# A linear-attention block with a feed-forward layer, rewritten into one written instruction order

## The chip, the cores and the metric

The kernel runs on one core of one Trainium2 chip. The metric is the device time of one execution in microseconds (us). Before the change it was 351.17 us, the median of five runs (350.06 to 351.9).

The engines are PE (matmul; PEld is its weight load, which overlaps it), DVE (the vector engine), ACT (the scalar engine), POOL (the general-purpose engine) and SP (which issues DMAs). Lines such as L338 refer to the source of the kernel that the profile belongs to. In the changed kernel L299 is a projection (V or K), L338 the K normalisation, L378 the Q projection, L417 the attention matmul, L478 the output projection, L552 the feed-forward up projection and L570 the down projection. A few experiments shift these numbers by a few lines; the names of the tiles stay.

## The reference

The input has 2048 tokens of 640 values, 32 heads of 20, and a hidden width of 1728. Everything is bf16 at the borders.

```
xn = layernorm(x);  q, k, v = xn @ wqkv            # 32 heads of 20
pq = q @ w_phi ; pk = k @ w_phi                    # per head, 20x20
phi_q = [softmax(pq), softmax(-pq)]                # 40 features per head
phi_k = [softmax(pk), softmax(-pk)]
kv = phi_k^T @ v ;  z = sum over tokens of phi_k
o = (phi_q @ kv) / (phi_q @ z + 1e-6)
h = x + o @ wo
out = h + silu(layernorm(h) @ w1) @ w2
```

## The kernel before

It works in stages over 16 tiles of 128 tokens. First it folds w_phi into the Q and K weights, with transposes of the weights on PE. Then comes the K pass:

```
psv = Xn @ Wv ; psk = Xn @ Wfk                     # PE, 640 wide, as 512 + 128 columns
Ek[..., 0:20] = exp(+psk), exp(-psk)               # ACT, heads padded from 20 to 32
nc.vector.tensor_reduce(Sk[:], Ekb[:, :, 0:DH], axis=AX.X, op=ALU.add)       # L258
nc.vector.reciprocal(Sk[:], Sk[:])                                           # L259
nc.vector.tensor_tensor(Ekb[:, :, 0:DH], ..., Sk broadcast, op=ALU.mult)     # L260
for p in range(16):
    nc.tensor.matmul(kv[:, p, 0:42], Ek[:, p*128:(p+1)*128], Vp[:, p, 0:42]) # 2 heads each
... (cut)
```

The Q pass does the same normalisation for Q (L369 to L371), transposes the 2048 padded exponentials with 16 PE transposes and two ACT copies (L388, L398), multiplies by kv, divides, transposes again, applies `wo`, adds the residual as further matmuls against the identity, and normalises. After the Q pass the feed-forward part runs alone, in four blocks of 512 tokens: up projection, ACT sigmoid, DVE multiply by its input, down projection, DVE addition. The framework's scheduler orders the instructions of every engine.

The softmax here doesn't subtract the row's maximum and nothing guards it: scores larger than these inputs give would overflow.

Of the kernel before, what the change touches and what calls it, by code (L numbers as in the profile page):

```python
# [10 lines left out]
AX = mybir.AxisListType  # L11

BF16 = mybir.dt.bfloat16
F32 = mybir.dt.float32


@with_exitstack
def kernel(
# [14 lines left out]
    T = 16  # L33
    S = T * P
# [5 lines left out]
    FC = 14  # L40
    EPS = 1e-5

    x_t = A_x.rearrange("b (t p) d -> p (b t) d", p=P)
    out_t = out.rearrange("b (t p) d -> p (b t) d", p=P)

    persist = ctx.enter_context(tc.tile_pool(name="persist", bufs=1))
    early = ctx.enter_context(ExitStack())
    lnp = early.enter_context(tc.tile_pool(name="ln1", bufs=1))
    fp_ = early.enter_context(tc.tile_pool(name="fold", bufs=1))
    fps = early.enter_context(tc.tile_pool(name="foldps", bufs=2, space=bass.MemoryType.PSUM))  # L50
    lns = early.enter_context(tc.tile_pool(name="ln1s", bufs=3))
    lnps = early.enter_context(tc.tile_pool(name="ln1ps", bufs=2, space=bass.MemoryType.PSUM))
# [3 lines left out]
    eps_t = persist.tile([P, 1], F32, name="eps_t")  # L56
    nc.gpsimd.memset(eps_t[:], EPS)
    nhalf_t = persist.tile([P, 1], F32, name="nhalf_t")
    nc.gpsimd.memset(nhalf_t[:], -0.5)

    wqkv_sb = fp_.tile([P, C, 3 * D], BF16, name="wqkv_sb")
    wqkv_v = A_wqkv.rearrange("(c p) n -> p c n", p=P)
    nc.sync.dma_start(wqkv_sb[:, :, 1 * D : 2 * D], wqkv_v[:, :, 1 * D : 2 * D])
    WPH = fp_.tile([DH, H, DH], BF16, name="WPH")
    nc.scalar.dma_start(WPH[:], A_w_phi.rearrange("h d f -> d h f"))
    X_sb = lnp.tile([P, T, D], BF16, name="X_sb")
    for g4 in range(4):
        nc.gpsimd.dma_start(
            X_sb[:, 4 * g4 : 4 * (g4 + 1), :], x_t[:, 4 * g4 : 4 * (g4 + 1), :]
        )  # L70
    for i in (2, 0):
        nc.sync.dma_start(wqkv_sb[:, :, i * D : (i + 1) * D], wqkv_v[:, :, i * D : (i + 1) * D])
    wo_sb = persist.tile([P, C, D], BF16, name="wo_sb")
    nc.sync.dma_start(wo_sb[:], A_wo.rearrange("(c p) n -> p c n", p=P))
    XT = persist.tile([P, C, S], BF16, name="XT")
    for c in range(C):
        nc.sync.dma_start_transpose(XT[:, c, :], A_x[0, :, c * P : (c + 1) * P])

    SID = fp_.tile([DH, 3 * P], BF16, name="SID")
    nc.gpsimd.memset(SID[:], 0.0)  # L80
    nc.vector.tensor_copy(SID[:, P : P + DH], ident[0:DH, 0:DH])
    phi_sb = fp_.tile([P, C, D], BF16, name="phi_sb")
    for r in range(C):
        pphi = fps.tile([P, H, 32], F32, name="psw")
        heads = []
        for h in range(H):
            r0 = DH * h
            if r0 // P != r and (r0 + DH - 1) // P != r:
                continue
            p0 = r0 - r * P  # L90
            heads.append((h, p0))
        for (h, p0) in heads:
            nc.tensor.matmul(
                pphi[:, h, 0:DH],
                SID[:, P - p0 : 2 * P - p0],
                WPH[:, h, :],
                start=True,
                stop=True,
            )
        h_lo = heads[0][0]  # L100
        h_hi = heads[-1][0] + 1
        if h_lo > 0:
            nc.gpsimd.memset(phi_sb[:, r, 0 : DH * h_lo], 0.0)
        if h_hi < H:
            nc.gpsimd.memset(phi_sb[:, r, DH * h_hi : D], 0.0)
        nc.scalar.copy(
            phi_sb[:, r, DH * h_lo : DH * h_hi].rearrange("p (h f) -> p h f", f=DH),
            pphi[:, h_lo:h_hi, 0:DH],
        )

    Wfq = persist.tile([P, C, D], BF16, name="Wfq")
    Wfk = persist.tile([P, C, D], BF16, name="Wfk")
    Wv = persist.tile([P, C, D], BF16, name="Wv")
    XnT = persist.tile([P, C, S], BF16, name="XnT")

    nc.vector.tensor_copy(Wv[:], wqkv_sb[:, :, 2 * D : 3 * D])

    WTs = {}
    for which in (1, 0):
        base = which * D  # L120
        WT = fp_.tile([P, C, D], BF16, name=f"WT{which}")
        for r in range(C):
            pwt = fps.tile([P, C, P], BF16, name="pwt")
            for ce in range(C):
                nc.tensor.transpose(  # L125
                    pwt[:, ce, :],
                    wqkv_sb[:, ce, base + r * P : base + (r + 1) * P],
                    ident[:],
                )
            nc.scalar.copy(WT[:, r, :], pwt[:].rearrange("p a b -> p (a b)"))  # L130
        WTs[which] = WT

    Xn = lnp.tile([P, T, D], BF16, name="Xn")

    def ln1_group(g):
        for tt in range(8):
            t = g * 8 + tt
            stats = lns.tile([P, 2, 6], F32, name="st1")
            for i in range(2):
                nc.vector.bn_stats(stats[:, i, :], X_sb[:, t, i * 320 : (i + 1) * 320])  # L140
            mv = lns.tile([P, 2], F32, name="mv1")
            nc.vector.bn_aggr(mv[:], stats[:])
            rstd = lns.tile([P, 1], F32, name="rstd1")
            nc.vector.tensor_scalar_add(rstd[:], mv[:, 1:2], EPS)
            nc.gpsimd.tensor_tensor(rstd[:], rstd[:], nhalf_t[:], op=ALU.pow)
            nmr = lns.tile([P, 1], F32, name="nmr1")
            nc.vector.tensor_scalar(
                out=nmr[:], in0=mv[:, 0:1], scalar1=rstd[:, 0:1], scalar2=-1.0,
                op0=ALU.mult, op1=ALU.mult,
            )  # L150
            nc.vector.tensor_scalar(
                out=Xn[:, t, :], in0=X_sb[:, t, :],
                scalar1=rstd[:, 0:1], scalar2=nmr[:, 0:1],
                op0=ALU.mult, op1=ALU.add,
            )
        for c in range(C):
            pst = lnps.tile([P, 8, P], BF16, name="pXT")
            for tt in range(8):
                t = g * 8 + tt
                nc.tensor.transpose(pst[:, tt, :], Xn[:, t, c * P : (c + 1) * P], ident[:])  # L160
            if g == 0:
                nc.vector.tensor_copy(
                    XnT[:, c, g * 8 * P : (g + 1) * 8 * P],
                    pst[:].rearrange("p a b -> p (a b)"),
                )
            else:
                nc.scalar.copy(
                    XnT[:, c, g * 8 * P : (g + 1) * 8 * P],
                    pst[:].rearrange("p a b -> p (a b)"),
                )  # L170

    def fold(which):
        Wf = Wfk if which == 1 else Wfq
        WT = WTs[which]
        for ce in range(C):
            psw = fps.tile([P, D], F32, name="psw")
            for n0, n1 in ((0, 512), (512, 640)):
                for r in range(C):
                    nc.tensor.matmul(  # L179
                        psw[:, n0:n1],  # L180
                        WT[:, r, ce * P : (ce + 1) * P],
                        phi_sb[:, r, n0:n1],
                        start=(r == 0),
                        stop=(r == C - 1),
                    )
            if which == 1:
                nc.scalar.copy(Wf[:, ce, :], psw[:])
            else:
                nc.vector.tensor_copy(Wf[:, ce, :], psw[:])  # L189

    ln1_group(0)
    fold(1)
    fold(0)
    ln1_group(1)
    early.close()

    wpool = ctx.enter_context(tc.tile_pool(name="wpool", bufs=1))
    w1_sb = wpool.tile([P, C, F], BF16, name="w1_sb")
    nc.sync.dma_start(w1_sb[:], B_w1.rearrange("(c p) n -> p c n", p=P))
    w2_sb = wpool.tile([P, FC, D], BF16, name="w2_sb")  # L200
    nc.sync.dma_start(
        w2_sb[:, 0:13, :], B_w2[0 : 13 * P].rearrange("(c p) n -> p c n", p=P)
    )
    nc.sync.dma_start(w2_sb[0:64, 13, :], B_w2[13 * P : F, :])
    HnT = wpool.tile([P, C, S], BF16, name="HnT")

    KVBD = persist.tile([P, 16, 42], BF16, name="KVBD")
    nc.vector.memset(KVBD[:], 0.0)
    p2pre_ctx = ctx.enter_context(ExitStack())
    p2pre = p2pre_ctx.enter_context(tc.tile_pool(name="p2pre", bufs=1))  # L210
    p1ctx = ctx.enter_context(ExitStack())
# [10 lines left out]
    def p1_stage_AB(t):  # L222
# [11 lines left out]
        for n0, n1 in ((0, 512), (512, 640)):  # L234
# [29 lines left out]
            op=ALU.mult,  # L264
        )
        ek_state[t] = Ek
        vp_state[t] = Vp

    def p1_stage_C(t):
        Ek = ek_state[t]  # L270
# [364 lines left out]
```

## Time and profile before

| stretch of the span (us) | what runs | PE busy | DVE busy | granted PE clock |
|---|---|---|---|---|
| 0 to 49 | loads, fold, LayerNorm | 32.58 of 49 | 33.02 | 1.00 |
| 62 to 118 | K pass | 50.03 of 56 | 54.24 | 1.00 |
| 118 to 213 | Q pass | 78.53 of 95 | 85.25 | 0.96 |
| 213 to 350.5 | feed-forward | 131.45 of 137.5 | 52.46 | 1.00 |

The table is taken from this view of the kernel before: busy time of each engine in stretches of the span. The columns are the stretch, its length, then each engine's busy us with its number of instructions in brackets, the granted clock, the mean busy share of the DMA engines, and GB/s.

```profile
core 0: us, PE busy (x) PEld busy (x) DVE busy (x) ACT busy (x) POOL busy (x), PEclk, DMA share, GB/s
0.00:49.00 49.00, 32.58 (x273) 20.33 (x274) 33.02 (x106) 14.95 (x25) 22.47 (x47) 1.00 0.64 175
...
62.00:118.00 56.00, 50.03 (x551) 29.04 (x548) 54.24 (x52) 32.73 (x50) 14.71 (x22) 1.00 0.17 63
118.00:213.00 95.00, 78.53 (x947) 52.93 (x948) 85.25 (x165) 67.16 (x89) 21.28 (x27) 0.96 0.01 2
213.00:350.50 137.50, 131.45 (x755) 61.45 (x753) 52.46 (x74) 39.34 (x62) 0.39 (x1) 1.00 0.06 20
```

The share of DVE moves from stage to stage, so no single engine bounds the kernel: DVE is the busiest in the K and Q passes, PE in the feed-forward part. The page of the kernel before says the same in its slices (the span in 40 equal parts, each digit the busy share in tenths) and in the chain of waits.

```profile
PE   2299878999996779788999767999999999999995
...
DVE  0985987999999999998989865441453145315421
```

```profile
PE 49%; DVE 33%; ACT 6%; DMA 4%; POOL 4%; issue 2%; SPq 0%; DVEq 0%; POOLq 0%; ACTq 0%
```

These are the groups of instructions of the kernel before that the change is about. After the bar come busy us and the mean ns of one, then idle time just before them.

```profile
L260 DVE TENSOR_TENSOR Ek<-Ek,Sk 128x1280 bf16<-128x1280 bf16 x16 | 23.7, 1483 | 1.4
L258 DVE TENSOR_REDUCE Sk<-Ek 128x64 f32<-128x1280 bf16 x16 | 23.6, 1476 | 2.4 <-ACT Ek L256 2.4
...
L371 DVE TENSOR_TENSOR Eq<-Eq,Sq 128x1280 bf16<-128x1280 bf16 x14 | 20.8, 1483 | 0.1
L369 DVE TENSOR_REDUCE Sq<-Eq 128x64 f32<-128x1280 bf16 x14 | 20.5, 1473 | 0.0
...
L388 ACT COPY EqT<-psT 128x1024 bf16<-128x1024 bf16 x16 | 16.3, 1017 | 11.7 <-PE psT L387 11.7
```

One tile of the K pass costs DVE 1.48 + 0.55 + 1.48 us, 3.51 us, and the step from one tile to the next in the chain is about 3.6 us, so DVE hardly pauses.

### The profile page before, as it was taken

What the parts mean: (1) busy time and instruction counts of PE and PEld (TensorE: products, weight loads), DVE (VectorE), ACT (ScalarE), POOL (GpSimd) and SP (SyncE); (2) the same over time, 40 slices, a digit from 0 to 9 for tenths busy, and PEclk for the clock granted to TensorE, in tenths of its full rate; (3) what the DMA queues carried; (4) which work ended last, traced back from release to release, by engine and by line L of the source; (5) the groups of instructions that cost most, each with busy time, mean ns of one, the idle gap of its engine ahead of it and who ended that gap; (6) DMA issues with size and microseconds to landing.
All of it is one profiled execution on the core that took longest, in us unless ns stands there. A gap on an engine that the chain in (4) does not pass through costs nothing.

```text
span 350.5 us, 6366 instructions
## 1 busy us (share of the span) xinstructions
PE 304.0 (87%) x2642; PEld 170.8 (49%) x2642; DVE 235.2 (67%) x407; ACT 165.0 (47%) x239; POOL 62.0 (18%) x101
## 2 busy tenths in 40 slices
PE   2299878999996779788999767999999999999995
PEld 2166445555554556555665443445544544444443
DVE  0985987999999999998989865441453145315421
ACT  3153049646466566776899455420742044104400
POOL 7430552333320012333231010000000000000000
PEclk9999999999999989999999899999999999999999
DMA  8995002910000000000000000001000100010011
GB/s 271 401 197 109 2 1 82 392 35 2 2 0 2 1 2 2 2 0 2 3 2 1 2 0 2 0 21 37 19 2 19 39 19 1 21 38 18 2 37 37
DMA packets 18997, 15.98 MB, mean 46 GB/s; under 512 B 11482, under 2 KB 17818, under 8 KB 18970
## 3 DMA queue, kind: packets, MB, share of 16 engines
q1 hardware_dynamic: 17744, 12.95, 12.7%
q0 software_dynamic: 576, 2.62, 1.8%
q8 instruction: 20, 0.33, 0.4%
q10 hardware_dynamic: 650, 0.03, 0.1%
q14 instruction: 7, 0.06, 0.1%
HBM read 10.35 MB, written 2.62 MB: 37 GB/s over the span
## 4 chain that ended last, share of the span: by engine, by line
PE 49%; DVE 33%; ACT 6%; DMA 4%; POOL 4%; issue 2%; SPq 0%; DVEq 0%; POOLq 0%; ACTq 0%
PE psy L587 19%; PE psh L569 17%; DVE Ek L260 6%; DVE Sk L258 6%; DMA wqkv_sb<-in_A_wqkv_dram 4%; DVE Sq L369 4%; PE psw L179 4%; PE psa L442 3%; DVE O L419 3%; DVE Sk L259 2%; DVE Eq L371 2%; DVE st L485 2%; POOL rstd L490 2%; PE psT L395 1%; PE psq L349 1%
## 5 line engine op out<-in xcount | busy, mean ns | idle before, releaser
L587 PE MATMUL psy<-w_sb,shT 128*128 128x512 bf16 (+2 forms) x448 | 73.0, 300 | 0.0
L569 PE MATMUL psh<-HnT,w_sb 128*128 128x512 bf16 (+1 forms) x280 | 67.4, 378 | 2.4 <-DVE shT L578 1.7
L578 DVE TENSOR_TENSOR shT<-psh,sg 128x512 bf16<-128x512 f32 (+1 forms) x56 | 38.6, 691 | 38.3 <-ACT sg L577 38.3
L577 ACT ACTIVATE sg<-psh 128x512 bf16<-128x512 f32 (+1 forms) x56 | 33.3, 597 | 65.7 <-PE psh L569 57.8
L587 PEld LDWEIGHTS <-shT 128*128 128x128 bf16 (+1 forms) x448 | 33.7, 97 | 35.2 <-issue 10.4
L569 PEld LDWEIGHTS <-w_sb 128*128 128x128 bf16 (+1 forms) x280 | 26.7, 98 | 36.3 <-issue 8.4
L595 DVE TENSOR_TENSOR o_t<-psy,H_sb 128x640 bf16<-128x640 f32 x16 | 13.2, 825 | 43.4 <-PE psy L587 43.4
L442 PE MATMUL psa<-wo_sb,OT 128*128 128x512 bf16 (+1 forms) x160 | 29.4, 314 | 0.5 <-ACT OT L434 0.5
L236 PE MATMUL p1mm<-Wfk,XnT 128*128 128x512 bf16 (+1 forms) x160 | 26.4, 298 | 1.2 <-ACT Ek L256 0.4
L226 PE MATMUL p1mm<-Wv,XnT 128*128 128x512 bf16 (+1 forms) x160 | 25.0, 299 | 1.1 <-DVE Wfq L189 1.0
L349 PE MATMUL psq<-Wfq,XnT 128*128 128x128 bf16 (+1 forms) x140 | 24.0, 298 | 2.0 <-ACT Eq L362 1.7
L258 DVE TENSOR_REDUCE Sk<-Ek 128x64 f32<-128x1280 bf16 x16 | 23.6, 1476 | 2.4 <-ACT Ek L256 2.4
L260 DVE TENSOR_TENSOR Ek<-Ek,Sk 128x1280 bf16<-128x1280 bf16 x16 | 23.7, 1483 | 1.4
L388 ACT COPY EqT<-psT 128x1024 bf16<-128x1024 bf16 x16 | 16.3, 1017 | 11.7 <-PE psT L387 11.7
L255 ACT ACTIVATE Ek<-p1mm 128x640 bf16<-128x640 f32 x16 | 11.3, 704 | 20.5 <-PE p1mm L236 17.2
L371 DVE TENSOR_TENSOR Eq<-Eq,Sq 128x1280 bf16<-128x1280 bf16 x14 | 20.8, 1483 | 0.1
L369 DVE TENSOR_REDUCE Sq<-Eq 128x64 f32<-128x1280 bf16 x14 | 20.5, 1473 | 0.0
L359 POOL MEMSET Eq<- 128x768 bf16 x14 | 10.3, 744 | 56.0 <-PE psT L395 50.5
L140 DVE BATCH_NORM_STATS2 st<-X_sb 128x6 f32<-128x320 bf16 x32 | 14.3, 465 | 8.1 <-DMA X_sb<-in_A_x_dram 8.1
L398 ACT COPY EqT<-psT 128x1024 bf16<-128x1024 bf16 x16 | 16.2, 1016 | 7.3 <-PE psT L395 7.2
L490 POOL TENSOR_TENSOR rstd<-rstd,nhalf_t 128x1 f32<-128x1 f32 x16 | 13.5, 846 | 34.8 <-DVE rstd L489 34.5
L125 PE MATMUL pwt<-ident,wqkv_sb 128*128 128x128 bf16 x50 | 6.7, 307 | 13.7 <-DMA wqkv_sb<-in_A_wqkv_dram 13.0
(91 smaller groups left out, 457.8 us busy)
## 6 DMA issues: line engine op xcount, KB each, us to landing
X_sb<-in_A_x_dram POOLq DMA_DIRECT2D x4, 640.0 KB, 9.4
out_dram<-o_t SPq DMA_DIRECT2D x16, 160.0 KB, 1.8
wqkv_sb<-in_A_wqkv_dram SPq DMA_DIRECT2D x3, 800.0 KB, 11.0
w_sb<-in_B_w_dram SPq DMA_DIRECT2D x1, 2160.0 KB, 8.2
w_sb<-in_B_w_dram SPq DMA_DIRECT2D x1, 2080.0 KB, 13.9
wo_sb<-in_A_wo_dram SPq DMA_DIRECT2D x1, 800.0 KB, 16.6
XT<-in_A_x_dram SPq DMA_TRANSPOSE x5, 5.4
w_sb<-in_B_w_dram SPq DMA_DIRECT2D x1, 80.0 KB, 13.5
```

Of the source, the lines that this page charges most:

```text
L226: nc.tensor.matmul(psv[:, n0:n1], XnT[:, c, t * P : (t + 1) * P], Wv[:, c, n0:n1], start=(c == 0), stop=(c == C - 1),)
L236: nc.tensor.matmul(psk[:, n0:n1], XnT[:, c, t * P : (t + 1) * P], Wfk[:, c, n0:n1], start=(c == 0), stop=(c == C - 1),)
L258: nc.vector.tensor_reduce(Sk[:], Ekb[:, :, 0:DH], axis=AX.X, op=ALU.add)
L260: nc.vector.tensor_tensor(Ekb[:, :, 0:DH], Ekb[:, :, 0:DH], Sk[:].unsqueeze(2).to_broadcast([P, 64, DH]), op=ALU.mult,)
L349: nc.tensor.matmul(psq[:, n0:n1], XnT[:, c, t * P : (t + 1) * P], Wfq[:, c, n0:n1], start=(c == 0), stop=(c == C - 1),)
L369: nc.vector.tensor_reduce(Sq[:], Eqb[:, :, 0:DH], axis=AX.X, op=ALU.add)
L371: nc.vector.tensor_tensor(Eqb[:, :, 0:DH], Eqb[:, :, 0:DH], Sq[:].unsqueeze(2).to_broadcast([P, 64, DH]), op=ALU.mult,)
L442: nc.tensor.matmul(psa[:, n0:n1], OT[:, c, :], wo_sb[:, c, n0:n1], start=(c == 0), stop=False,)
L569: nc.tensor.matmul(psh[0:rows, :], w1_sb[:, c, fc * P : fc * P + rows], HnT[:, c, q * 512 : (q + 1) * 512], start=(c == 0), stop=(c == C - 1),
L577: nc.scalar.activation(sg[0:rows, :], psh[0:rows, :], AF.Sigmoid)
L578: nc.vector.tensor_tensor(shT[0:rows, fc, :], psh[0:rows, :], sg[0:rows, :], op=ALU.mult)
L587: nc.tensor.matmul(psy[:, n0:n1], shT[0:rows, fc, si * P : (si + 1) * P], w2_sb[0:rows, fc, n0:n1], start=(fc == 0), stop=(fc == FC - 1),)
```

## The change

The kernel is rewritten. Its intent is to take work off PE and DVE, and to fill every gap of PE with work of another stage. The core of the diff, with cuts:

```diff
+ORDER = """
+mk st.1 st.0 rs.1 xn.1 rs.0 xn.0 xt.0 xc.0.v st.2 xt.1 xc.1 vp.0 vc.0 vp.1 vc.1 wt.0 wc.0.a st.3
+... (cut: one word for each operation of each tile, about 60 lines)
+"""
 # K normalisation: heads stay 20 wide, and the multiply moves to POOL
-nc.vector.tensor_tensor(Ekb[:, :, 0:DH], ..., Sk broadcast, op=ALU.mult)
+n = H if t == T - 1 else 2 * H           # the last tile is shared with DVE
+nc.gpsimd.tensor_tensor(Ek3[:, 0:n], Ek3[:, 0:n], Sk broadcast, op=ALU.mult)
 # K.V: 64 columns of Ek against 4 heads of V, 20 matmuls of 84 columns a tile
-nc.tensor.matmul(tgt[:, pi, 0:42], Ek[:, p*P:(p+1)*P], Vp[:, p, 0:42], ...)
+nc.tensor.matmul(kv[s][lo:lo+64, r], Ek[:, s, 64*q:64*q+64], Vp[:, HQ[q]:HQ[q]+4, :], ...)
 # Q: exponentials made transposed, so no transposes and no normalisation of Q
+nc.tensor.matmul(ps[:, k, :], Wfq[:, c, r*P:(r+1)*P], XnT[g][:, c, :], ...)       # qp
+nc.scalar.activation(E[:, s, ...], ps, AF.Exp, scale=1.0 - 2.0 * s)               # qe
 # attention for one half of the heads; the two softmaxes are combined afterwards (DVE)
+nc.tensor.matmul(ps[:, s, ...], EqT[g][:, s, r, i*P:(i+1)*P], KVBD[:, s, r, ...])  # dp
+w = sum0/sum1 ; u = A1*w + A0                                                     # dw
+o = u[..., 0:20] * (1/u[..., 20])                                                 # do
 # residual on DVE, with the sum for the LayerNorm; the squares on ACT
-nc.tensor.matmul(psa[:, c_lo:c_hi], XT[:, c, ...], ident[...])
+nc.vector.scalar_tensor_tensor(out=Xv, in0=ps, in1=Xv, ..., accum_out=st[:, 0:1])  # oa
+nc.scalar.activation(sq[:], X[:, t, :], AF.Square, accum_out=st[:, 1:2])           # sq
 # some transposes go through DRAM (words xs/xd, ts/td, hs/hd), the others stay on PE
+nc.sync.dma_start(os_[:], o) ; nc.sync.dma_start_transpose(ot[:], os_[:])
 # feed-forward
-sigmoid on ACT, multiply on DVE
+nc.scalar.activation(sh, ps, AF.Silu)
+# the last chunk of 64 rows is padded with zeros to 128
+# 14 matmuls on zeros run while the first loads are under way
+with tc.manual_schedule(engines={PE, SP, POOL, DVE, ACT}):
+    for word in ORDER.split(): ops[name](*args)
```

Each engine executes its instructions in the order of the words. In that order, feed-forward operations (up, ua, yp, yo) stand among the attention operations of later tiles.

## The prediction

> **What bounds the kernel now.** Stages with different limits. The table of busy time by stretch shows: 0 to 49 us (loads, folding, LayerNorm) PE busy only 33; 62 to 118 us, the K pass, DVE 54.2 of 56; 118 to 213 us, the Q pass, DVE 85.3 of 95; then the FFN, PE 131 of 138. The chain of waits agrees: PE 49%, DVE 33%, ACT 6%. In the K pass the chain is a DVE loop of about 3.6 us a tile: reduce 1.48, reciprocal 0.55, broadcast multiply 1.48. In the Q pass DVE, ACT and PE hand work around through short buffers.
>
> In the chain ten 512-column matmuls take 2.22 us, so PE streams about 2.35 columns a nanosecond. I count 625,000 columns, an estimated 264 us: some 85 of 350 us are PE idleness.
>
> **What the change does.** A rewrite in one hand-fixed instruction order.
> - PE columns fall to about 575,000 (my count), an estimated 240 to 244 us: Q's exponentials are made already transposed (33,000 go); the fold uses only non-zero head blocks (32,000 to 7,000); the residual is added on DVE (10,000 less); some transposes go to DMA. K.V grows to 27,000, attention to 25,000.
> - DVE loses the K multiply (23.7 us, to POOL) and the Q normalisation (reduce 20.5, reciprocal 7.4, multiply 20.8), replaced by combining both halves after the matmul, an estimated 1.9 us per half tile, 61 us. DVE falls from 235 to roughly 160 us.
> - ACT loses the sigmoid step (one Silu), the 32 transposed copies (32.5 us) and H copies; it gains squares.
> - POOL gains the K multiply. The Trainium skill, "GPSIMD Engine Reference", section 3.1, states about 2.6 cycles per element at 1.2 GHz for a two-input op; 1280 elements make an estimated 2.8 us. The old trace has no such instruction. 15.5 of them are 43 us, plus small ops.
>
> **Critical path, by stage.** First real PE work at about 8 us (the first weight landed at 6.2 before), first K projection about 21 us. PE then has 55 us of K-pass work, but POOL, from its first multiply (about 26 us), needs 54: the pass, with the masked KV copies on DVE, ends near 84 us against 118; PE loses some 8 us. The rest is about 408,000 columns, 174 us; with FFN work interleaved into attention I allow 9 us of stalls. The tail (last add and store), about 4 us, stays. 84 + 174 + 9 + 4 = 271 us.
>
> **Prediction: 271 us, 259 to 290 in 8 of 10 cases.** Faster by over 2%: 0.98; within 2%: 0.01; slower: 0.01.
>
> **What would show each step.** Table of engines: fewer PE instructions, DVE about 160 us, POOL well over 100. Groups by line: the POOL multiply near 2.8 us; no 128x1024 ACT copies. Slices: PE at 9 in nearly all slices after 84 us. Chain of waits: PE over 75%, POOL between 26 and 84 us, DVE under 10%. First attention matmul near 84 us.
>
> **What would make it wrong.** A POOL multiply at 3.5 us, or DVE and POOL slowing each other, would cost 10 us or more; at 2 us the K-pass stall vanishes. The 18 round trips through DRAM for transposes share one in-order queue (before, a transpose of 16 blocks held it about 5.6 us); if it blocks, PE idles in the FFN. A denser PE could be granted a lower clock (mean 0.99; 0.96 in the Q pass). The start, some 20 us of small dependent steps, could be slower.

## The result

The changed kernel takes 262.04 us, the median of 8 runs (261.81 to 262.91), against 351.21 us. The ratio is 0.7461 with a 95% interval from 0.7447 to 0.7476. A ratio is always the mean time of one kernel's fast runs over that of the other's fast runs of the same rounds, so it is not quite the ratio of the medians.

This is the stretch view of the changed kernel, cut where its stages begin: the first K projection (21.8 us), the first attention matmul (81.4 us), and the last matmul (257.4 us).

```profile
0.00:21.80 21.80, 16.81 (x139) 10.51 (x140) 15.12 (x42) 10.42 (x15) 11.72 (x43) 1.00 0.97 323
21.80:81.40 59.60, 55.75 (x669) 38.01 (x667) 44.09 (x67) 43.00 (x64) 50.79 (x63) 1.00 0.26 70
81.40:257.40 176.00, 175.47 (x1295) 115.75 (x1295) 97.42 (x255) 65.62 (x94) 22.25 (x80) 1.00 0.21 59
257.40:261.20 3.80, 0.00 (x0) 0.00 (x0) 0.82 (x1) 0.00 (x0) 0.00 (x0) 0.95 0.12 43
```

After 81.4 us PE is busy 175.47 of 176.00 us, while attention and feed-forward work of different tiles alternate. The slices of the changed kernel show the same, and the granted clock stays at the top digit in all of them:

```profile
PE   7789998999997999999999999999999999999994
...
DVE  4689999377648894689787333994735605332012
...
PEclk9999999999999999999999999999999999999999
```

DVE is at 9 in eight of the 40 slices. PE busy went from 304.0 to 248.0 us and PE idle from 46.5 to 13.2 us (span less busy). Busy time includes modelled pipeline ends, so the split is rough. DVE busy went from 235.2 to 157.5 us, ACT from 165.0 to 119.0, and POOL from 62.0 to 84.8. The K reduce is still there, the multiply is now on POOL, and no group for the Q normalisation remains:

```profile
L338 POOL TENSOR_TENSOR Ek<-Ek,Sk 128x1280 bf16<-128x1280 bf16 x15 | 35.0, 2356 | 0.8 <-DVE Sk L331 0.8
...
L328 DVE TENSOR_REDUCE Sk<-Ek 128x64 f32<-128x1280 bf16 x16 | 23.4, 1460 | 7.5 <-ACT Ek L320 7.4
```

Finally, these are the longest waits of PE in the changed kernel: who waited for whom, us in total, times, longest.

```profile
PE mm L417 <- DVE KVBD L370: 1.8, 1, 1.8
PE q L245 <- DVE xn L234: 1.8, 2, 1.5
PE q L599 <- POOL ident masks.py:199: 1.5, 1, 1.5
PE mm L299 <- ACT Vp L309: 1.3, 1, 1.3
PE kv L351 <- POOL Ek L338: 0.6, 1, 0.6
```

KVBD is the masked copy of the K.V sums that the attention matmuls read. PE waits for POOL's multiply only 0.6 us in all. The chain of waits of this profile could not be read as hoped: it is followed back only to 160 us, and its shares add up to 38% of the span (PE 31%).

### The profile page after: what moved, and what is told of

It reads as the page before. It is cut to its first block, busy times and chain, and to the rows that moved or that the text cites. A ratio compares the mean times of both kernels' runs of the same rounds, so it can differ in the third digit from the quotient of the medians.

```text
span 261.2 us, 5215 instructions
## 1 busy us (share of the span) xinstructions
PE 248.0 (95%) x2099; PEld 164.3 (63%) x2099; DVE 157.5 (60%) x363; ACT 119.0 (46%) x172; POOL 84.8 (32%) x186
## 5 line engine op out<-in xcount | busy, mean ns | idle before, releaser
L552 PE MATMUL mm<-HnT,w 128*128 128x512 bf16 (+1 forms) x350 | 63.7, 337 | 0.0
L570 PE MATMUL mm<-w,shT 128*128 128x320 bf16 x448 | 63.5, 299 | 0.0
L570 PEld LDWEIGHTS <-shT 128*128 128x128 bf16 x448 | 43.5, 98 | 16.8
L563 ACT ACTIVATE shT<-mm 128x1024 bf16<-128x1024 f32 (+1 forms) x29 | 28.4, 992 | 54.0 <-PE mm L552 53.8
L552 PEld LDWEIGHTS <-w 128*128 128x128 bf16 x350 | 33.6, 98 | 23.6 <-issue 0.2
L299 PEld LDWEIGHTS <-XnT 128*128 128x128 bf16 x320 | 30.4, 98 | 14.1 <-issue 2.0
L338 POOL TENSOR_TENSOR Ek<-Ek,Sk 128x1280 bf16<-128x1280 bf16 (+1 forms) x16 | 36.9, 2329 | 2.1 <-DVE Sk L331 2.1
L299 PE MATMUL mm<-wv,XnT 128*128 128x320 bf16 x160 | 24.2, 300 | 1.9 <-ACT Vp L309 1.3
L478 PE MATMUL mm<-wo,ot 128*128 128x320 bf16 x160 | 24.2, 299 | 0.4 <-DMA ot<-os 0.4
L299 PE MATMUL mm<-Wfk,XnT 128*128 128x320 bf16 x160 | 23.9, 299 | 0.2 <-ACT Ek L320 0.2
```

Source lines behind the costliest of these rows:

```text
L299: nc.tensor.matmul(ps[:, half, 0:320], tok(XnT[t // GT], t)[:, c, :], W[:, c, half * 320 : (half + 1) * 320], start=(c == 0), stop=(c == C ...
L338: nc.gpsimd.tensor_tensor(Ek3[:, 0:n], Ek3[:, 0:n], Sk[:, 0:n].unsqueeze(2).to_broadcast([P, n, DH]), op=ALU.mult,)
L478: nc.tensor.matmul(ps[:, half, 0:320], tl["ot", t][:, c, :], wo[:, c, half * 320 : (half + 1) * 320], start=(c == 0), stop=(c == C - 1),)
L552: nc.tensor.matmul(ps[:, i, 0:W], w1[:, c, fc * P : (fc + 1) * P], HnT[g][:, c, 0:W], start=(c == 0), stop=(c == C - 1), skip_group_check= ...
L563: nc.scalar.activation(sh[:, a:b, 0:W], tl["up", g, k][:, 0 : b - a, 0:W], AF.Silu)
L570: nc.tensor.matmul(tl["yp", t][:, half, 0:320], shT[g][:, fc, i * P : (i + 1) * P], late["w2"][:, fc, half * 320 : (half + 1) * 320], star ...
```

## The experiments

Twelve kernels were run, each an edit of the changed kernel, in three groups, each group on one chip and beside runs of the kernel before (median 350.8 to 351.3 us each time). Because the changed kernel itself was timed in another session, experiments are compared with it through their ratios to the kernel before (0.7461 for the changed kernel), and microseconds are differences of medians. Where PE waited more, its mean granted clock in the profiled run was lower too (0.994 in e5, 0.991 in e2 and e3, 0.983 in e10, 0.964 in e9, 0.904 in e11, 0.882 in e1, against 0.999), so the losses of these runs contain some slower matmuls. All results are correct except e12, which is wrong on purpose.

| run | median us | ratio (95% interval) | against 262.04 |
|---|---|---|---|
| e7_double_dp | 272.48 | 0.7769 (0.7746 to 0.7792) | +10.4 |
| e10_dve_load | 294.45 | 0.8402 (0.8364 to 0.8439) | +32.4 |
| e2_k_on_dve | 272.31 | 0.7758 (0.7726 to 0.7791) | +10.3 |
| e5_k_split | 266.75 | 0.7598 (0.7571 to 0.7625) | +4.7 |
| e12_k_half_work | 261.68 | 0.7468 (0.744 to 0.7497) | -0.4, no difference by ratio |
| e1_ffn_last | 338.69 | 0.9648 (0.9598 to 0.9698) | +76.7 |
| e11_ffn_last_pe | 339.97 | 0.9694 (0.9667 to 0.9721) | +77.9 |
| e3_pe_transposes | 282.93 | 0.8051 (0.8021 to 0.8081) | +20.9 |
| e9_auto | 280.74 | 0.7995 (0.7972 to 0.8018) | +18.7 |
| e6_no_warm | 264.05 | 0.7531 (0.7504 to 0.7558) | +2.0 |
| e8_half_chunk | 267.35 | 0.7615 (0.7597 to 0.7633) | +5.3 |
| e13_half_chunk_fullk | 262.04 | 0.7468 (0.7447 to 0.7488) | 0.0 |

### Is PE the limit now?

The first theory is that time now follows PE's columns. The rival is that PE only looks busy and really waits for others.

```diff
-        for s in range(2):                # op_dp
+        for s in (0, 0, 1, 1):            # every attention matmul twice, same result
```

> Each of the 192 attention matmuls is issued twice with the same result: 25,300 more columns and nothing else on any engine. Theory A (PE streams without gaps from about 90 us on, so time follows its columns): six of them took 0.35 us in the chain, 32 groups make 11.2 us, about 273 us. Rival B (PE has slack there and waits for others): under 266 us.

It took 10.4 us more for 25,300 more columns (my count; the weights of these matmuls are loaded again too), 2.4 columns a nanosecond, the rate at which PE streams in the chain. So in the second part a column of PE costs its full time. The rival falls.

### Did the relief of DVE matter?

```diff
+        # in op_dw, for each half tile: a scratch tile that nobody reads
+        nc.vector.tensor_reduce(dsum[:], dload[:] as 32 x 20, axis=AX.X, op=ALU.add)
+        nc.vector.tensor_tensor(dload[:], dload[:], dsum broadcast, op=ALU.mult)
```

> For each of the 32 half tiles of attention, VectorE gets back the kind of work that the change took from it: a reduce and a broadcast multiply over 640 elements of a scratch tile that nobody reads, an estimated 1.6 us each time and 51 us in all (half of 1.46 us and half of 1.49 us, rounded up for the fixed part). Result unchanged. Theory A (the relief of VectorE in the attention pass was needed: PE works in a fixed order and waits where VectorE is late): PE waits for VectorE between 90 and 150 us, 275 us or more. Rival B (after the K pass VectorE is busy 100 of 180 us, so there is room): under 266 us.

DVE's busy time rose by 47.2 us (157.5 to 204.7), the total by 32.4 us, although DVE is busy only 97 of the 176 us after the K pass in the changed kernel. The longest waits of PE in this experiment:

```profile
PE mm L466 <- DVE o L456: 9.4, 7, 2.6
PE mm L562 <- DVE u L440: 2.6, 4, 1.4
PE mm L533 <- DVE hn L524: 2.4, 2, 1.3
```

PE stands at a fixed place in its order until DVE delivers `o`. The load stands between `u` and `o`, on the very path that PE waits for, so e10 shows what work costs there, and not what 47 us elsewhere on DVE would cost. On that path an average busy share of 55% was no room to spare. The removed Q normalisation (48.7 us in the three groups of the kernel before) is thus likely a large part of the gain. How large can't be said, because an order made for the heavier DVE might hide more of it.

### What limits the K pass?

Three runs vary who multiplies K. In the changed kernel the first attention matmul starts at 81.4 us.

```diff
-        n = H if t == T - 1 else 2 * H ; nc.gpsimd.tensor_tensor(Ek3[:, 0:n] ...)
+        e2:  n = 2 * H ; nc.vector.tensor_tensor(Ek3[:, 0:n] ...)      # all on DVE
+        e5:  n = H for every t: POOL one half, DVE the other
+        e12: n = H for every t: POOL one half, nobody the other (DVE only for the last tile)
```

> The multiply that normalises the K exponentials goes back from POOL to VectorE for all 16 tiles. Theory A (moving it was needed, the K pass would be VectorE-bound again): VectorE has about 43 us of work between 22 and 80 us and gets 23 us more, 66 us for 58 us of time: the first attention matmul moves from 81 to about 89 us and the total to about 270 us. Rival B (VectorE had room, POOL was the limit): no loss, total 258 to 263 us.

> The K multiply is shared half and half by POOL and VectorE for every tile, so that POOL is relieved by some 15 us or less. Theory of the prediction (POOL and PE nearly tie in the K pass, PE loses about 8 us to it): the first attention matmul comes up to 5 us earlier, total 257 to 259 us. Rival (the measured 2.36 us a tile leaves POOL room, PE's own columns limit the K pass): 261 to 264 us, no gain.

> Wrong result on purpose: POOL multiplies only the first half of the K exponentials of each tile, and VectorE does not take the other half, so POOL has some 15 us less to do in the K pass and no engine more. Theory of the prediction (POOL and PE nearly tie in the K pass): the first attention matmul comes 3 to 5 us earlier than 81.4 us, total 257 to 259 us. Rival (PE's own columns and the start limit the K pass): at most 1 us earlier, 261 to 262.5 us.

With everything on DVE (e2) the first attention matmul came at 90.6 us and the total rose by 10.3 us, close to the 8 us expected. In this order, moving the multiply was needed.

The split (e5) made it worse (85.5 us, +4.7 us), against both expectations. The two multiplies hold each other up. First e12, where POOL multiplies half as much and DVE (except on the last tile) nothing, then two POOL instructions and one DVE instruction of e5 (start, duration, instruction), and last all the multiplies of e5:

```profile
L338 POOL TENSOR_TENSOR Ek<-Ek,Sk x16: 1270/1272/1915, 28.2 to 75.3; 128x640 bf16<-128x640 bf16 x16
```

```profile
28.60 1.27 POOL L338 TENSOR_TENSOR Ek<-Ek,Sk 128x640 bf16<-128x640 bf16 x1
...
31.33 1.90 POOL L338 TENSOR_TENSOR Ek<-Ek,Sk 128x640 bf16<-128x640 bf16 x1
```

```profile
31.28 0.82 DVE L342 TENSOR_TENSOR Ek<-Ek,Sk 128x640 bf16<-128x640 bf16 x1
```

```profile
L338 POOL TENSOR_TENSOR Ek<-Ek,Sk x16: 1266/1844/1915, 28.6 to 80.0; 128x640 bf16<-128x640 bf16 x16
...
L342 DVE TENSOR_TENSOR Ek<-Ek,Sk x16: 770/825/1885, 27.0 to 79.9; 128x640 bf16<-128x640 bf16 x16
```

A half multiply takes POOL 1.27 us alone (minimum, median and maximum ns are the three numbers after the count). Read one by one in e5, of two multiplies that overlap the one that starts later takes longer: 11 of the 16 POOL multiplies start while DVE's runs and take 1.84 to 1.92 us; four DVE multiplies start while POOL's runs and take 1.12 to 1.89 us, against 0.77 to 0.83 us for the other twelve. So the split leaves POOL most of its old 2.36 us and gives DVE more work, at times slowed. The Trainium skill's page "GPSIMD Engine Reference", section 1 (Specifications), says that POOL shares its SBUF interfaces with the vector engine, with contention from DVE instructions with two SBUF inputs; this trace agrees, with the durations above.

e12 tells whether POOL mattered at all: POOL's busy time fell by 16.0 us, and the first attention matmul came at 80.8 in place of 81.4 us, with no difference in the total. These lines give the attention matmuls of the changed kernel, then of e12, with the first and the last start after the durations:

```profile
L417 PE MATMUL mm<-KVBD,EqT x192: 201/228/233, 81.4 to 223.2; 128*128 128x154 bf16 x128, 128*128 128x88 bf16 x64
```

```profile
L417 PE MATMUL mm<-KVBD,EqT x192: 199/228/233, 80.8 to 221.9; 128*128 128x154 bf16 x128, 128*128 128x88 bf16 x64
```

POOL had room, and the prediction's account, in which POOL's 54 us set the end of the K pass, is refuted. PE itself was busy 55.75 of the 59.60 us there. That its own matmuls limit this pass is read from this; no run changes PE's work in the K pass alone.

### What does the interleaving do?

In e1 all feed-forward words are moved behind the last attention word.

```diff
+ORDER = [words other than up, ua, yp, yo] + [words up, ua, yp, yo]
-        tc.tile_pool(name="hntp", bufs=2, side="right")
+        tc.tile_pool(name="hntp", bufs=5, side="right")
```

> The changed kernel's same work, but every feed-forward operation is moved behind the last attention operation (and five buffers for the transposed second LayerNorm instead of two). Theory A (the interleaving hides the attention pass's VectorE work behind feed-forward matmuls): after the K pass at about 81 us, VectorE has some 83 us of attention work that no feed-forward matmul covers, then 121 us of feed-forward and 4 us of tail follow: about 288 us, 26 us over the changed kernel. Rival B (only the smaller work counts, the order little): under 268 us. PE idle should appear between 97 and 165 us.

It lost 76.7 us, three times what I expected. PE stood 32.3 us waiting for the transposes that go through DRAM, so I suspected those, and e11 makes all of them on PE instead, in the same stage-wise order.

> As e1_ffn_last (all feed-forward work behind the attention pass), but all 18 DRAM round trips are PE transposes with ScalarE copies. Tells what made e1_ffn_last lose 77 us. Theory A (exposed DRAM round trips, where PE stood 32 us in e1, are its main loss, and the rest is VectorE's attention work of about 83 us): about 295 us, between 285 and 305. Rival B (the attention pass without feed-forward work between is slow for another reason, such as PE waiting for VectorE and POOL at each LayerNorm, and a lower granted clock): above 315 us.

That did not help (339.97 us), so the rival's forecast was the right one: without the DRAM trips the pass is as slow. (e11 also has four buffers in place of two for `o` and `hn`, and puts the transposes into PE's order, so it doesn't tell what the trips alone cost e1.) PE now waits for DVE instead, and in both runs the granted clock falls in the stretch without feed-forward work. First the two largest waits of PE in e11, then the slices of e1:

```profile
PE mm L457 <- DVE o L447: 26.4, 14, 4.4
PE mm L524 <- DVE hn L515: 16.1, 7, 4.1
```

```profile
PE   7789899997997577545465042999999999999995
...
PEclk9999999999999875767655565899999999999999
```

The mean granted clock was 0.882 in e1 and 0.904 in e11, against 0.999. An output projection of ten matmuls that takes 1.52 us in the changed kernel took 2.85 us in e1:

```profile
181.61 2.85 PE L479 MATMUL mm<-wo,ot 128*128 128x320 bf16 x10 [2.40 <-DMA ot<-os]
```

The Trainium skill, "TensorE: Matmul & The Clock Gate", section "Why this matters for your kernels", says to leave no idle gaps of more than about 3 us between bursts of matmuls, or the clock drops to half. The trace agrees in kind: the clock falls to 5 to 8 tenths where PE is half idle. It doesn't agree in size. The clock records kept in the trace are only full or half (the slices are averages), and the first fall in e1 is at 115.7 us, when no gap of PE since 82 us had been longer than 1.9 us: starts of the 320-column matmuls are 0.136 us apart before it and 0.267 us after. So a gap of 3 us was not needed here; how much idleness is enough stays open. One tile's steps (attention, combine, transpose, project, LayerNorm) hang on each other, and without foreign work between them PE waits, and then also runs slower.

The 77 us are not the worth of interleaving as such. This order was made for the interleaved program; a stage-wise order with its own software pipeline might do better: the old Q pass, with other work in it, took 95 us, and the stretch between the K pass and the feed-forward part in e1 about 130. The runs show what feed-forward work does in this order: it fills the waits.

### Do the transposes through DRAM pay?

```diff
-ts.t ... td.t    and    hs.t ... hd.t       (store to DRAM, transposed load)
+tp.t tc.t        and    hp.t hc.t           (at the place of td/hd; 17 of 18)
-        name="o", bufs=2 ; name="hn", bufs=2
+        name="o", bufs=4 ; name="hn", bufs=4
```

> 17 of the 18 transposes that go through DRAM in the second half are made on PE again, with a copy on ScalarE (5 transposes of 128 columns each). Theory A (PE is the limit there, and time follows its columns): 10,880 more columns, 4.5 us more, about 266.5 us. Rival B (the DRAM round trips hold PE up): the same or faster, 258 to 262 us.

It lost 20.9 us, far more than the 4.5 us of columns. One of the 18 was left as it was, because the program deadlocked in simulation otherwise. PE was busy 8.0 us longer (256.0 us) and idle 11.6 us longer (24.8 us). In e3 ACT stands in its own order until the PE transpose is there, and PE until DVE's `o` is:

```profile
ACT HnT L529 <- PE mm L524: 36.3, 9, 6.8
```

```profile
PE mm L457 <- DVE o L447: 5.0, 2, 2.7
```

So both theories missed it. My reading, which no run tests alone: a PE transpose puts a wait into the orders of PE and ACT; the DRAM trip waits in SP's queue, where little else waits. The waits shown are only a part of the loss. What remains open, too, is how much of this a new order for the PE version would win back. e3 used the places of the old one.

### What is the written order worth?

```diff
-    with tc.manual_schedule(engines={PE, SP, POOL, DVE, ACT}):
+    if True:                              # the framework's scheduler, as before the change
```

> The same program, but the framework's scheduler orders each engine's instructions, as in the kernel before, instead of the written order. Theory A (the fixed order is worth much: PE was 95% busy with it): PE falls under 90%, 272 us or more. Rival B (a scheduler that sees the same program finds as good an order): 262 to 266 us.

It is worth 18.7 us here. The first attention matmul came at 97.0 us, 15.6 us later than 81.4, so most of it is lost early: from there to the end of the span e9 needs 183.9 us and the changed kernel 179.8. These are the largest waits of PE in e9:

```profile
PE mm L299 <- DVE XnT L158: 9.5, 1, 9.5
PE q L245 <- DVE xn L234: 6.4, 1, 6.4
```

There the scheduler placed POOL's preparation of KVBD (needed at about 78 us in the changed kernel) at 12.7 us, in front of small POOL steps of the first LayerNorms; the written order has it at 62.0 us. This placement is one visible difference and was not tested alone. The waits also cost clock: the trace has it at half from 11.4 to 28.4 us, and the first ten V projections take 2.85 us there.

### What are the matmuls on zeros for?

```diff
-        for i in range(14):
-            nc.tensor.matmul(warm_ps[:], ident[:], warm[:], start=True, stop=True)
```

> The 14 matmuls on zeros that run before any data has landed are left out. Theory A (they only keep PE busy so that the first real matmuls run at full speed): the matmuls from 8 to about 12 us run at half the speed, 1 to 2 us are lost, of which waits on the loads absorb a part: 262.5 to 264 us. Rival B (they are useless, the start is bound by loads and LayerNorm): the same time within 0.3 us.

It lost 2.0 us, at the upper end of theory A. The first V projections, 20 matmuls, in the changed kernel and then in e6 (start, duration):

```profile
8.88 2.89 PE L299 MATMUL mm<-wv,XnT 128*128 128x320 bf16 x20 [0.31 <-DVE XnT L158]
```

```profile
9.12 4.59 PE L299 MATMUL mm<-wv,XnT 128*128 128x320 bf16 x20
```

A PE that had not worked yet took 1.7 us more for the same matmuls. This agrees with the advice on the same page of the Trainium skill ("TensorE: Matmul & The Clock Gate", Part 1) that full speed comes only after a few us of sustained work. The stretch view reads 1.00 for the granted clock here in both kernels, but only because it takes a stretch without a clock record as full: the first record in the trace, of full speed, comes at 4.83 us in the changed kernel and at 12.63 us in e6. Read one by one, the V projections of e6 start 0.267 us apart up to 12.56 us and 0.136 us apart soon after, while all of them start about 0.136 us apart in the changed kernel.

### Two attempts at a faster kernel

The last feed-forward chunk has 64 rows, padded to 128. Side by side in two column halves of the array, the two halves of the tokens could share the array.

```diff
+ if fc == FC - 1:      # up: two token halves at once, 64 output rows each
+     nc.tensor.matmul(ps[64*b : 64*b+64, i, 0 : W//2], w1[:, c, fc*P : F], HnT[g][:, c, half b])
  # down, last chunk:
+ e8:  lhsT = shT[64*b : 64*b+64, 13, ...], rhs = w2[64*b : 64*b+64, 13, ...]     # 64 rows
+ e13: lhsT = shT[0:128, 13, ...], rhs = w2[:, 13 + b, ...]   # 128 rows, other half zeros
+ e13: the last output tile is added and stored in two halves
```

> An attempt at a faster kernel. The last feed-forward chunk has only 64 rows; its two halves of the tokens are put side by side in the two column halves of the array (64 columns each) and run side by side, half as many columns. Theory A (two 64-wide matmuls overlap, as the K.V matmuls appear to do at 25 ns each for 84 columns): 5,120 columns less, 2.1 us: about 260 us. Rival B (they don't overlap, or the weight loads of 64 columns cost as much): 262 us or more.

> A second attempt at a faster kernel. As e8_half_chunk, where the 64-row weights of the last down-projection chunk made each run of 14 matmuls take 2.10 us in place of 1.90: now that chunk is used with all 128 rows, against two copies of the 64 rows of the second weight, one padded with zeros below, one above. The last output tile is added and stored in two halves. Expected if the switch to 64-row weights was the loss: the up-projection gain of some 2 us stays, and the tail gains 0.3 us: 259.5 to 260.2 us. Otherwise 262 us or more.

e8 was slower by 5.3 us. The up projection gained: two 64-wide matmuls of 256 columns overlap. But a run of 14 down-projection matmuls, the last of them with 64-row weights, takes 2.10 us from its start to the next instruction's start, against 1.90 in the changed kernel (starts at 196.26 and 198.36, and at 192.24 and 194.14). Over 32 such runs that is 6.4 us. Read one by one, the extra time is at the two changes of shape: about 0.1 us between the starts into the 64-row matmul (0.232 in place of 0.136 us) and 0.1 us out of it (0.238). The first fence is of e8, the second of the changed kernel.

```profile
196.26 2.17 PE L585 MATMUL mm<-w,shT 128*128 128x320 bf16 x14
198.36 1.53 PE L477 MATMUL mm<-wo,ot 128*128 128x320 bf16 x10
```

```profile
192.24 2.06 PE L570 MATMUL mm<-w,shT 128*128 128x320 bf16 x14
194.14 0.51 PE L417 MATMUL mm<-KVBD,EqT 128*128 128x154 bf16 x6
```

The zero padding of the changed kernel is thus worth having. e13 avoids the 64-row weights and ends at 262.04 us, no different from the changed kernel. It keeps only part of the up-projection gain (one such group of 20 matmuls takes 4.00 in place of 4.32 us). It gives the rest back at new waits: 0.83 us for a transposed load, which PE now reaches earlier, and 0.58 us where the second half of the last tile waits for the addition of its first half:

```profile
255.28 2.06 PE L587 MATMUL mm<-w,shT 128*128 128x320 bf16 x14 [0.58 <-DVE obh L595]
```

That last wait I brought in myself: both halves lie in one PSUM tile (that the tile is tracked as a whole is my reading, not a test). So no version here beats the changed kernel.

A further experiment, going back from Silu to sigmoid and multiply, deadlocked in simulation with this order and was not run. What that part of the change is worth stays open.

## Why the prediction was right

The time (262.04 us against 271, range 259 to 290) and the direction were right. Point by point:

- **Bound before.** The stages were read correctly. e2 and e10 agree: DVE work put back into the changed kernel's K pass or on its attention path costs 10 and 32 us.
- **Start.** First K projection at 21.8 us, predicted about 21; first real PE work at 7.84, predicted about 8.
- **K pass.** Predicted end 84 us, measured 81.4. Its reason, that POOL "needs 54" us and that "PE loses some 8 us", was wrong; that its end came within 3 us is partly luck. PE was idle 3.9 us there (59.60 less 55.75). The multiply took 2.36 us and not the estimated 2.8, and e12 shows that even half of it would change nothing. Of PE's idle time, 1.8 us is the wait for the masked KV copies and 1.3 us a wait for a V copy (the list of waits); POOL's share is 0.6 us. The K.V matmuls were also over-counted: I took 84 columns each at full width, 11.2 us in all, but 20 of them take about 0.5 us of PE's order (starts at 72.10 and 72.60 in the trace), an estimated 8 us for 16 tiles. The trace's first POOL multiply starts at 28.2 us, predicted about 26.
- **Rest.** Predicted 174 us of columns and 9 us of stalls, 183 us; measured 176.0 us. This is the term that was mis-sized: the columns held (e7 confirms their price), and the stalls were some 2 us instead of 9 (176.0 less 174; the wait view has 0.5 us of PE idleness there).
- **Tail.** 3.8 us, predicted about 4.
- **The signs in the profile.** DVE busy 157.5 us (predicted about 160), PE at 9 in nearly all slices: right. POOL "well over 100" was wrong, 84.8, with the multiply at 36.9 us in place of 43; for the small steps the prediction gave no figure. The chain of waits, predicted at over 75% PE, could not be judged, as it reaches only the last 38%.
- **The risks.** None cost much: the clock stayed at 0.999, POOL was slowed by DVE only on the last tile, which they share (its half multiply took 1.91 us in place of 1.27), the queue of DRAM transposes held PE up for 0.4 us, and the start was not slower.

Where the 89 us came from cannot be split into parts that add up, for the parts lean on each other: fewer columns (at e7's price an estimated 21 us for the 50,000 columns less), a lighter DVE (e10: 32 us for 47 us of work put on its attention path), the place of the K multiply (10 us), and an order without holes (e9: 19 us).

## What to carry to other kernels

When an in-order engine is to stay busy, look for work of another stage to put between dependent steps, and then judge the other engines by when they deliver and not by their mean busy share: here 47 us more work on an engine busy 55% of the time, put on the path that PE waited for, cost 32 us. Before sharing one operation between POOL and DVE, measure both at once, since the one that started second was slowed (POOL from 1.27 to as much as 1.92 us, DVE from 0.82 to as much as 1.89). Price a change on a saturated PE by its columns, but check changes of the weights' shape separately: going to one 64-row matmul and back cost 0.2 us each time, more in all than the zeros that it saved.

## What the Trainium skill lacked or had wrong

- "GPSIMD Engine Reference", section 3.1, has about 2.6 cycles per element for a two-input op, measured on an fp32 addition. Here a bf16 multiply with a broadcast f32 operand took 2356 ns for 1280 elements and 1272 ns for 640, which is 1.69 ns, or 2.0 cycles at the page's 1.2 GHz, for each further element. So the figure was too high for this form.
- "TensorE: Matmul & The Clock Gate" and "TensorEngine Tiling (Array Packing)" have no cost for going from weights of one shape to another and back. Here one 64-row matmul in a run of 14 added 0.20 us (2.10 against 1.90 us in e8), about 0.1 us for each change. A group of 64-column matmuls shows the same: the step into it was 0.31 in place of 0.22 us and the step out 0.21 in place of 0.11 us (e13, from 221.47 us).
- "TensorE: Matmul & The Clock Gate", Part 3, gives a measured gain for column tiles of 32 only. Here ten 64-wide matmuls of 256 columns ran as five pairs, 3 to 4 ns apart within a pair and 106 ns from one pair to the next, which is the full factor of two inside the group. With the last step out the ten took 0.67 us to the next start (221.47 to 222.14 in e13), where the five of 512 columns that they replace take an estimated 1.08 us at the rate of the chain.
